# Two sums of a decode attention kernel, streamed through column tiles of the PE array instead of loaded as weights

## The chip, the cores and the metric

The kernel runs on one core of one Trainium2 chip. The metric is the device time of one execution in microseconds (us). Executions of one kernel agree within about 0.3%, so medians of several runs are given, and ratios with a 95% interval. A ratio is the mean time of one kernel's runs over the mean of the other's from the same rounds on the same chip, so it is not quite the ratio of the medians that stand beside it.

In the profiles PE is the matmul engine (TensorE) and PEld its weight loads, DVE is VectorE, ACT is ScalarE, POOL is GpSimd, and SP is SyncE, which issues most of the transfers here; `q` after a name means its instruction queue. SBUF is the on-chip memory, PSUM the one that matmuls write.

## The reference

The forward pass of a block for one decoded token, and its gradient with respect to everything. The part that matters:

```python
# x: [1, 1, 640]; k_cache, v_cache: [1, 32, 8192, 128] bf16 (32 heads, 8192 positions, 128 wide)
q = (xn @ wq)                                   # 32 heads of 128
scores = einsum("bhqd,bhkd->bhqk", q, k) * 128 ** -0.5
p = softmax(scores)
o = einsum("bhqk,bhkd->bhqd", p, v)             # "o sum"
out = x + o.reshape(...) @ wo + mlp(xn)         # ... cut
# and jax.vjp of this with grad_out. Per head, with do = wo-part of grad_out:
#   dv = p (outer) do;  ds = p * (do.v - sum(p * do.v));  dk = ds (outer) q;  dq = ds . k   # "dq sum"
```

K and V are read and dK and dV written once: 32 heads x 4 tensors of 2 MiB. That is 268 of the 305 MB that move.

## The kernel before

Position `s = 64 p + j` of a head lies on partition `p`, column block `j`, so a head's K or V is one SBUF tile of 128 partitions x 16 KiB. Ten such tiles (slots) circulate. Loads and stores of these tiles all go out on one queue (SP), in program order; a new load needs a slot whose store has landed:

```python
def store(kind, h):
    t = kv_tiles.pop((kind, h))
    # ... (cut)
    fifo((dkc if kind == "K" else dvc)[h], t[:])      # fifo = nc.sync.dma_start
    free_slots.append(t)
    load_next()                                       # loads into free_slots.pop(0)
```

PE transposes K and V in chunks (`T`, fp32 transposes of pairs of bf16, evicted from PSUM by ACT), and the transposed chunks are the weights of 64-column matmuls that give the scores and `do.v` (`M`). DVE writes the outer products dV and dK over the V and K tiles. The part that changes is the pair of sums over positions. It loads each 128x128 block of V (K) as weights and multiplies it by one column of p (ds), repeated over 64 columns:

```python
def o_sum(h, lo, hi):
    # ... (cut)
    for j in range(lo, hi):                            # 64 blocks in all
        nc.tensor.matmul(S_["hb"][:, 0:RW], lhsT=V3[:, j, :], rhs=S_["P2"][:, j, 0:1].to_broadcast([P, RW]),
                         start=(j == 0), stop=(j == J - 1), skip_group_check=True)

def dq_sum(h):
    # ... (cut)
    for j in range(J):
        nc.tensor.matmul(S_["hb"][:, RW:2 * RW], lhsT=K3[:, j, :], rhs=S_["U2"][:, j, 0:1].to_broadcast([P, RW]),
                         start=False, stop=(j == J - 1), skip_group_check=True)
    nc.scalar.copy(grp[g]["od"][:, hh, :], S_["hb"][:, RW - 1:RW + 1])
```

In a head the order was: `o_sum` first half, `dsum` (the scalar sum(p * do.v) for ds), `o_sum` second half, `dq_sum`.

## Time and profile before

749.35 us, median of 3 runs (748.56 to 749.82); the profiled execution spans 745.6 us.

| what | measured | where it is read |
|---|---|---|
| DMA share, 20 to 700 us | 0.99 to 1.02 | windows |
| PE / DVE / ACT busy | 80% / 60% / 45% | page, part 1 |
| SP waits for stores to land / for DVE's products | 544 us / 32 us | waits of SP |
| one DMA engine alone at the end | 731 to 744.2 us | windows |
| instructions of PE and PEld | 22,526 = 88.0 x 256 | page, part 1 |
| 16 KiB packets of the instruction queue q8 | 88 | page, part 3 |

The page of the kernel before: the span, busy times with instruction counts, the DMA's busy tenths and GB/s in 40 slices of 18.6 us, and the two queues that fetch instructions (packets, MB, share of 16 engines).

```profile
span 745.6 us, 25013 instructions
...
PE 596.1 (80%) x11263; PEld 568.4 (76%) x11263; DVE 447.8 (60%) x739; ACT 333.4 (45%) x668; POOL 30.4 (4%) x45
...
DMA  8999999999999999999999999999999999999991
GB/s 327 387 413 421 426 425 425 395 427 426 416 426 427 428 421 428 425 428 425 424 424 429 426 425 417 415 417 424 420 413 425 418 417 419 419 415 418 408 402 72
...
q8 instruction: 88, 1.44, 0.7%
...
q14 instruction: 20, 0.16, 0.1%
```

DMA is at 9 (90% or more) in every slice but the first and the last. "q8 instruction" and "q14 instruction" are not data: they are instructions being fetched.

The groups of instructions of the kernel before that the change touches or leans on: busy us and mean ns of one, then idle time before them and what ended it.

```profile
L274 PE MATMUL pT<-ident_f,kv 128*128 128x128 f32 x2048 | 337.1, 289 | 67.4 <-DMA kv<-in_A_k_cache_dram 62.4
L276 ACT COPY KT<-pT 128x512 f32<-128x512 f32 x512 | 299.3, 586 | 182.6 <-PE pT L274 149.4
...
L358 PE MATMUL hb<-P,kv 128*128 128x64 bf16 x2048 | 82.3, 202 | 14.3 <-DVE U L365 14.3
...
L373 PE MATMUL hb<-U,kv 128*128 128x64 bf16 x2048 | 70.8, 194 | 5.1 <-issue 5.1
```

A busy time of overlapping matmuls overstates their cost: in the timeline, from the start of a sum to the start of what PE does next, its 64 matmuls take 2.1 us (o, in two halves) and 1.95 us (dq). The first line shows PE idle for 62 us in front of transposes, waiting for K to arrive. PE waits for DMA, not the other way round.

The waits of the SP queue before (total us, times, longest), which issues the K and V transfers:

```profile
SPq L101 <- DMA out_dram<-kv: 543.6, 57, 16.9
SPq L101 <- DVE kv L379: 31.9, 11, 7.2
...
SPq L749 <- DMA out_dram<-fin_bf: 15.1, 1, 15.1
```

SP spends 544 us waiting for stores to land before it may reuse a slot, and only 32 us for DVE's outer products.

Windows of the kernel before. Columns: the stretch, its length, busy us and count of PE, PEld, DVE, ACT and POOL, the PE clock granted, the DMA share of 16 engines, GB/s.

```profile
300.00:320.00 20.00, 14.49 (x275) 13.84 (x274) 13.09 (x19) 8.93 (x18) 0.00 (x0) 0.98 1.01 427
720.00:731.00 11.00, 0.93 (x3) 0.59 (x3) 7.29 (x28) 0.00 (x0) 1.63 (x2) 0.50 0.85 346
731.00:736.00 5.00, 0.00 (x0) 0.00 (x0) 0.00 (x0) 0.00 (x0) 0.00 (x0) 0.50 0.06 26
736.00:741.00 5.00, 0.00 (x0) 0.00 (x0) 0.00 (x0) 0.00 (x0) 0.00 (x0) 0.50 0.06 25
```

A share of 0.06 is 1/16. From 731 us on one DMA engine works alone, at the 26 GB/s that one engine moves, with all other engines of the core finished. The timeline of the kernel before agrees (start, length, engine, instruction; the last three entries):

```profile
728.63 0.28 DVE L721 CAST fin_bf<-pT 10x128 bf16<-10x128 f32 x1 [0.56 <-PE pT L719]
728.94 0.54 ACTq L722 DMA_DIRECT2D out_dram<-fin_bf  x1
729.52 0.28 ACTq L723 DMA_DIRECT2D out_dram<-fin_bf  x1
```

The last result is sent at 729.8 us, 16 us before the end.

### The profile page before, as it was taken

What the parts mean: (1) busy time and instruction counts of PE and PEld (TensorE: products, weight loads), DVE (VectorE), ACT (ScalarE), POOL (GpSimd) and SP (SyncE); (2) the same over time, 40 slices, a digit from 0 to 9 for tenths busy, and PEclk for the clock granted to TensorE, in tenths of its full rate; (3) what the DMA queues carried; (4) which work ended last, traced back from release to release, by engine and by line L of the source; (5) the groups of instructions that cost most, each with busy time, mean ns of one, the idle gap of its engine ahead of it and who ended that gap; (6) DMA issues with size and microseconds to landing.
All of it is one profiled execution on the core that took longest, in us unless ns stands there. A gap on an engine that the chain in (4) does not pass through costs nothing.

```text
span 745.6 us, 25013 instructions
## 1 busy us (share of the span) xinstructions
PE 596.1 (80%) x11263; PEld 568.4 (76%) x11263; DVE 447.8 (60%) x739; ACT 333.4 (45%) x668; POOL 30.4 (4%) x45
## 2 busy tenths in 40 slices
PE   1987698999999779888787897778798788979920
PEld 1886598988998778877686896778798787869820
DVE  4169937677767456656555763646556664656580
ACT  1641055555565355535355553445454353554500
POOL 0100200000000100001000000000000000000000
PEclk9997799999999889999999999998999899988965
DMA  8999999999999999999999999999999999999991
GB/s 327 387 413 421 426 425 425 395 427 426 416 426 427 428 421 428 425 428 425 424 424 429 426 425 417 415 417 424 420 413 425 418 417 419 419 415 418 408 402 72
DMA packets 29136, 304.63 MB, mean 409 GB/s; under 512 B 2836, under 2 KB 5972, under 8 KB 12644
## 3 DMA queue, kind: packets, MB, share of 16 engines
q1 hardware_dynamic: 22736, 276.39, 88.5%
q0 software_dynamic: 5984, 26.30, 8.8%
q8 instruction: 88, 1.44, 0.7%
q10 hardware_dynamic: 308, 0.33, 0.1%
q14 instruction: 20, 0.16, 0.1%
HBM read 151.67 MB, written 151.34 MB: 406 GB/s over the span
## 4 chain that ended last, share of the span: by engine, by line
DMA 48%; PE 39%; DVE 8%; issue 2%; ACT 1%; SPq 0%; ACTq 0%; DVEq 0%
DMA kv<-in_A_k_cache_dram 31%; PE pT L274 17%; DMA out_dram<-kv 13%; PE hb L358 6%; PE hb L373 4%; PE sA L293 4%; DMA kv<-in_A_v_cache_dram 4%; PE dA L293 4%; DVE kv L379 3%; DVE U L365 1%; PE sA L320 1%; PE dh_ps L462 1%; PE hb L363 1%; PE acc L536 1%; PE gu_ps L451 1%
## 5 line engine op out<-in xcount | busy, mean ns | idle before, releaser
L274 PE MATMUL pT<-ident_f,kv 128*128 128x128 f32 x2048 | 337.1, 289 | 67.4 <-DMA kv<-in_A_k_cache_dram 62.4
L276 ACT COPY KT<-pT 128x512 f32<-128x512 f32 x512 | 299.3, 586 | 182.6 <-PE pT L274 149.4
L274 PEld LDWEIGHTS pT<-ident_f,kv 128*128 128x128 f32 x2048 | 224.6, 145 | 71.5 <-issue 69.6
L293 PEld LDWEIGHTS <-KT 128*128 128x128 bf16 x4096 | 196.8, 100 | 17.7 <-issue 10.6
L379 DVE TENSOR_TENSOR kv<-qd,U 128x4096 bf16<-128x4096 bf16 x64 | 146.0, 2284 | 0.0
L379 DVE TENSOR_TENSOR kv<-qd,P 128x4096 bf16<-128x4096 bf16 x64 | 143.4, 2282 | 0.0
L293 PE MATMUL dA<-cz,KT 128*128 128x64 bf16 x2048 | 107.6, 197 | 8.0 <-ACT qd L310 5.8
L293 PE MATMUL sA<-cz,KT 128*128 128x64 bf16 x2048 | 102.7, 192 | 0.4 <-issue 0.3
L358 PEld LDWEIGHTS <-kv 128*128 128x128 bf16 x2048 | 81.7, 106 | 16.5 <-issue 16.5
L358 PE MATMUL hb<-P,kv 128*128 128x64 bf16 x2048 | 82.3, 202 | 14.3 <-DVE U L365 14.3
L375 ACT COPY od_g<-hb 128x2 f32<-128x2 f32 x32 | 5.1, 160 | 160.9 <-PE hb L373 160.9
L373 PE MATMUL hb<-U,kv 128*128 128x64 bf16 x2048 | 70.8, 194 | 5.1 <-issue 5.1
L373 PEld LDWEIGHTS <-kv 128*128 128x128 bf16 x2048 | 66.9, 98 | 6.0 <-issue 5.8
L349 DVE SCALAR_TENSOR_TENSOR U<-dA,P 128x64 bf16<-128x64 f32 x32 | 7.4, 232 | 93.7 <-PE dA L293 93.7
L316 DVE TENSOR_REDUCE mrow<-sA 128x1 f32<-128x64 f32 x32 | 7.2, 224 | 79.5 <-PE sA L293 79.5
L365 DVE SCALAR_TENSOR_TENSOR U<-dA,hb,P 128x128 bf16<-128x128 f32 x32 | 11.4, 355 | 36.3 <-PE hb L363 36.3
L429 DVE SCALAR_TENSOR_TENSOR wq_g<-wq_g,side 128x512 bf16<-128x512 bf16 x40 | 27.3, 683 | 0.0
L340 DVE RECIPROCAL rZ<-sA 128x1 f32<-128x1 f32 x32 | 5.4, 168 | 35.9 <-PE sA L334 35.0
L233 DVE SCALAR_TENSOR_TENSOR side<-wo_g,g_bc 128x640 bf16<-128x640 bf16 x32 | 26.2, 818 | 0.3
L323 DVE TENSOR_REDUCE negM<-sA 128x1 f32<-128x128 f32 x32 | 9.3, 291 | 18.6 <-PE sA L320 18.6
L424 POOL DMA_DIRECT2D out_dram<-wo_g x8 | 6.1, 761 | 295.5 <-DVE cz L298 262.3
L433 POOL DMA_DIRECT2D out_dram<-wq_g x8 | 6.9, 863 | 254.3 <-DVE wq_g L431 254.3
(134 smaller groups left out, 311.5 us busy)
## 6 DMA issues: line engine op xcount, KB each, us to landing
out_dram<-kv SPq DMA_DIRECT2D x64, 2048.0 KB, 31.8
kv<-in_A_k_cache_dram SPq DMA_DIRECT2D x32, 2048.0 KB, 26.9
kv<-in_A_v_cache_dram SPq DMA_DIRECT2D x32, 2048.0 KB, 26.9
out_dram<-wo_g POOLq DMA_DIRECT2D x8, 640.0 KB, 12.1
out_dram<-wq_g POOLq DMA_DIRECT2D x8, 640.0 KB, 13.3
wq_g<-in_A_wq_dram POOLq DMA_DIRECT2D x7, 640.0 KB, 13.8
wo_g<-in_A_wo_dram POOLq DMA_DIRECT2D x7, 640.0 KB, 19.5
kv<-in_B_w_dram SPq DMA_DIRECT2D x2, 1728.0 KB, 16.1
```

The costliest lines, as they stand in the source:

```text
L233: nc.vector.scalar_tensor_tensor(junk[:], G_["wo"][:, hh, :], 1.0, g_bc[:], ALU.mult, ALU.mult, accum_out=G_["do"][:, hh:hh + 1])
L274: nc.tensor.transpose(pT[:, k * P:(k + 1) * P], W3[:, 4 * c + k, :], ident_f[:])
L276: nc.scalar.copy(KT[:].rearrange("p k w -> p (k w)"), pT[:])
L293: nc.tensor.matmul(S_[kind][:, 0:J], lhsT=KTb[:, k, par, :], rhs=S_["cz"][:, o:o + J], start=(i == 0 and par == 0), stop=(par == 1), skip_ ...
L320: nc.tensor.matmul(S_["K"][:, J:J + P], lhsT=S_["mrow"][:].to_broadcast([P, P]), rhs=ident_f[:], start=False, stop=True, skip_group_check= ...
L323: nc.vector.tensor_reduce(S_["negM"][:], S_["K"][:, J:J + P], AX.X, ALU.max, negate=True)
L358: nc.tensor.matmul(S_["hb"][:, 0:RW], lhsT=V3[:, j, :], rhs=S_["P2"][:, j, 0:1].to_broadcast([P, RW]), start=(j == 0), stop=(j == J - 1), ...
L363: nc.tensor.matmul(S_["hb"][:, 2 * RW:2 * RW + 1], lhsT=negones_b, rhs=S_["rdot"][:], start=False, stop=True, skip_group_check=True)
L365: nc.vector.scalar_tensor_tensor(S_["U2"][:], S_["V"][:, 0:J].unsqueeze(2).to_broadcast([P, J, 2]), S_["hb"][:, 2 * RW:2 * RW + 1], S_["P2 ...
L373: nc.tensor.matmul(S_["hb"][:, RW:2 * RW], lhsT=K3[:, j, :], rhs=S_["U2"][:, j, 0:1].to_broadcast([P, RW]), start=False, stop=(j == J - 1) ...
L379: nc.vector.tensor_tensor(dst[:, lo * DH:hi * DH].rearrange("p (j a b) -> p j a b", a=DH // 2, b=2), vec.rearrange("p (a b) -> p a b", b=2 ...
L429: nc.vector.scalar_tensor_tensor(wq_g[:, ci, :], wq_g[:, ci, :], 1.0, dqb, ALU.mult, ALU.mult, accum_out=dxa[:, ci, g:g + 1])
```

## The change

The intent is to shorten PE's work: V and K stream as the moving operand in 512-column matmuls, four columns of p (ds) are the weights, and four such matmuls are to run at once, one in each 32-column tile of the array. Row m of a result then holds column m of the weights against four blocks of V, of which only block m is wanted; that diagonal is picked out later, by fp32 matvecs with 0/1 masks, after ACT has evicted the PSUM tile.

```diff
-    def o_sum(h, lo, hi):          # 64 matmuls, V blocks as weights (cut)
+    def wsum(h, kind, pair):
+        N4 = 4 * DH
+        W = kv_tiles[(kind, h)]
+        X = pst()
+        nc.tensor.matmul(X[:], lhsT=cz_tiles[0][:, 0:1].to_broadcast([P, P]), rhs=W[:, 0:N4], start=True, stop=False,
+                         skip_group_check=True)                          # zero weights: clears all 128 rows
+        for i in range(J // 4):
+            q = QW * (i % 4)                                             # QW = 32
+            nc.tensor.matmul(X[q:q + 4, :], lhsT=pair[:, 4 * i:4 * i + 4, 0], rhs=W[:, N4 * i:N4 * (i + 1)],
+                             start=False, stop=(i >= J // 4 - 4), skip_group_check=True)
+        XS = kt_tile()
+        nc.scalar.copy(XS[:].rearrange("p k w -> p (k w)"), X[:])
+        hd[h]["xs" + kind] = XS
...
     def dq_sum(h):
-        ...                        # 64 matmuls, K blocks as weights (cut)
+        wsum(h, "K", hd[h]["U2"])
+
+    def col(h, kind):
+        ...
+        for r in range(4):
+            nc.tensor.matmul(S_["hb"][:, a:a + 1], lhsT=XS[:, r, :], rhs=mask4[:, r:r + 1],
+                             start=False, stop=(r == 3), skip_group_check=True)
+        if a:
+            nc.scalar.copy(grp[g]["od"][:, hh, :], S_["hb"][:, 0:2])
...
         rdot(h)
-        o_sum(h, 0, J // 2)
+        o_sum(h)
         dsum(h)
-        o_sum(h, J // 2, J)
+        if pre:
+            T(h + 1, "K", 2)
         dq_sum(h)
```

`col` runs inside the next head, between its first score chunks. Loads, stores and DVE's work are as before.

More of the change, by code (lines that the diff above doesn't have):

```diff
@@ L160 @@
     nc.vector.tensor_copy(ident_bf[:], ident_f[:])
-    pm_one = consts.tile([P, 2], F32, name="pm_one")
+    masks = consts.tile([P, 8], F32, name="masks")
+    pm_one = masks[:, 0:2]
     nc.vector.memset(pm_one[:, 0:1], 1.0)
@@ L170 @@
     HW = P // 2
-    mask2 = consts.tile([P, 2], F32, name="mask2")
-    nc.vector.tensor_reduce(mask2[:], ident_f[:].rearrange("p (a b) -> p a b", b=HW), AX.X, ALU.add)
+    mask2 = masks[:, 2:4]
+    nc.vector.tensor_reduce(mask2, ident_f[:].rearrange("p (a b) -> p a b", b=HW), AX.X, ALU.add)
+    QW = P // 4
+    mask4 = masks[:, 4:8]
+    nc.vector.tensor_reduce(mask4, ident_f[:].rearrange("p (a b) -> p b a", b=QW)[:, 0:4, :], AX.X, ALU.add)
     sel = consts.tile([P, 2, P], BF16, name="sel")
@@ L255, in prep_cm @@
                                 ps.unsqueeze(2).to_broadcast([P, 4 * GH, 2]),
-                                mask2[:].unsqueeze(1).to_broadcast([P, 4 * GH, 2]), ALU.mult)
+                                mask2.unsqueeze(1).to_broadcast([P, 4 * GH, 2]), ALU.mult)
     hd = {}
@@ L350, in rdot @@
                                        accum_out=S_["rdot"][:])
-    def o_sum(h, lo, hi):
-        S_ = hd[h]
-        if lo == 0:
-            S_["hb"] = ps_h.tile([P, 2 * RW + 1], F32, name="hb", tag="hb")
-        V3 = kv_tiles[("V", h)][:].rearrange("p (j d) -> p j d", d=DH)
-        for j in range(lo, hi):
-            nc.tensor.matmul(S_["hb"][:, 0:RW], lhsT=V3[:, j, :], rhs=S_["P2"][:, j, 0:1].to_broadcast([P, RW]),
-                             start=(j == 0), stop=(j == J - 1), skip_group_check=True)
+    def wsum(h, kind, pair):
[11 more added lines that the diff above has]
+        hd[h]["xs" + kind] = XS
@@ L361, in dsum, with o_sum @@
+    def o_sum(h):
+        wsum(h, "V", hd[h]["P2"])
     def dsum(h):
         S_ = hd[h]
-        nc.tensor.matmul(S_["hb"][:, 2 * RW:2 * RW + 1], lhsT=negones_b, rhs=S_["rdot"][:], start=False, stop=True,
+        S_["hb"] = ps_h.tile([P, 4], F32, name="hb", tag="hb")
+        nc.tensor.matmul(S_["hb"][:, 2:3], lhsT=negones_b, rhs=S_["rdot"][:], start=True, stop=True,
                          skip_group_check=True)
         nc.vector.scalar_tensor_tensor(S_["U2"][:], S_["V"][:, 0:J].unsqueeze(2).to_broadcast([P, J, 2]),
-                                       S_["hb"][:, 2 * RW:2 * RW + 1], S_["P2"][:], ALU.add, ALU.mult)
+                                       S_["hb"][:, 2:3], S_["P2"][:], ALU.add, ALU.mult)
@@ L368, in dq_sum @@
     def dq_sum(h):
+        wsum(h, "K", hd[h]["U2"])
+    def col(h, kind):
         g, hh = divmod(h, GH)
         S_ = hd[h]
-        K3 = kv_tiles[("K", h)][:].rearrange("p (j d) -> p j d", d=DH)
-        for j in range(J):
-            nc.tensor.matmul(S_["hb"][:, RW:2 * RW], lhsT=K3[:, j, :], rhs=S_["U2"][:, j, 0:1].to_broadcast([P, RW]),
-                             start=False, stop=(j == J - 1), skip_group_check=True)
-        nc.scalar.copy(grp[g]["od"][:, hh, :], S_["hb"][:, RW - 1:RW + 1])
+        XS = S_.pop("xs" + kind)
+        a = 0 if kind == "V" else 1
+        for r in range(4):
[3 more added lines that the diff above has]
+            nc.scalar.copy(grp[g]["od"][:, hh, :], S_["hb"][:, 0:2])
@@ L617, in head @@
         has_prev = h > 0 and h != MLP_AT
-        had = 2 if h != MLP_AT else 0
+        had = (3 if h else 2) if h != MLP_AT else 0
         if nxt:
@@ L623, in head @@
         side_k(h)
+        if had == 3:
+            M(h, "K", 0)
         for c in range(had, NCH):
@@ L627, in head @@
                 M(h, "K", c - 2)
+            if has_prev and c == 3:
+                col(h - 1, "V")
+            if has_prev and c == 4:
+                col(h - 1, "K")
         T(h, "V", 0)
@@ L663, in head @@
         rdot(h)
-        o_sum(h, 0, J // 2)
+        o_sum(h)
         dsum(h)
-        o_sum(h, J // 2, J)
+        if pre:
+            T(h + 1, "K", 2)
         dq_sum(h)
+        if not pre:
+            col(h, "V")
+            col(h, "K")
     prep_new(0)
```

## The prediction

> **What bounds it now.** DMA. In the windows view the DMA share is 0.99 to 1.02 from 20 us to 700 us, at 398 to 432 GB/s, while PE is 80% busy and DVE 60%. PE sits idle 62 us in front of its transposes for K loads (groups view, L274). The SP queue waits 544 us for stores of K and V tiles before it may load again (waits of SP), and about 32 us for DVE's outer products.
>
> The end is peculiar. The last compute is at 729 us, the two tiny result stores go out at 729.5, yet the span is 745.6. From 731 to 744.6 the windows show DMA share 0.06 and 27 GB/s: one of 16 engines alone, finishing the last V and K stores in 16 KiB packets of 0.61 us. I put its extra work on PE's instruction fetch: queue 8 carries 88 packets of 16,384 bytes, each about 1.0 us. The Trainium skill, "Runtime: NRT & Kernel Launch", section "Instruction fetch mechanics", says refills are 16 KiB blocks of 256 instructions; the trace agrees: PE and PEld have 22,526 instructions, 88.0 blocks. Most fetches overlap one data packet lengthened by 0.3 to 0.6 us; 88 x about 0.38 us (estimate) = 33 us extra for that engine.
>
> **What the change does, per head.**
> - Removes 128 matmuls of 64 columns with their weight loads: 2.1 us for o and 1.95 us for dq in the chain.
> - Adds 2 zeroing matmuls and 32 four-wide ones over 512 columns. From L462 (384 columns, 0.266 us apart at clock 0.67) I estimate 0.24 us per 512 columns at full clock. Four tiles at once: 5 passes, 1.2 us per sum; serial: 17 passes, 4 us. The skill, "TensorE: Matmul & The Clock Gate", Part 3, gives 2.38x for three column tiles; no trace here shows it yet. I expect overlap, 1.2 to 1.8 us per sum.
> - Adds 8 fp32 mask matvecs, two passes each, at 0.12 us per fp32 pass (four transposes take 0.47 us): 1.9 us.
> - Adds two 128x512 evictions on ACT, 0.586 us each: 37 us in all, ACT 333 to about 370.
> - Moves one transpose chunk between the sums. DVE work, DMA bytes and load order stay.
>
> So PE gains no busy time (estimate 4.3 to 5.5 us against 4.05 per head), and it is off the critical path: a head needs about 17.5 us of PE against 21 us of DMA. What shrinks is the instruction stream: 22,526 to about 17,530, 88 to about 68.5 fetch blocks. 19.5 blocks x 0.38 us = 7 us off the lone engine's tail. The others end near 731 us: the floor.
>
> **Predicted: 742 us, range 735.5 to 750 (80%).** Faster by over 2%: 0.06. Within 2%: 0.87. Slower by over 2%: 0.07.
>
> **What would show it.** Right: queue 8 near 69 packets; the lone-engine stretch shrinks from 13.6 us to about 7; DMA share stays 1.0 at about 425 GB/s in the middle; PE busy within 10% of 596 us; DVE unchanged; each sum takes 1.2 to 1.8 us.
> Wrong: the lone-engine tail stays at 14 us with 69 fetches (fetch is not its cause); DMA share below 0.95 in the middle (PE or ACT paces it).
>
> **What would make it wrong.** If column tiles do not overlap, PE needs 22 to 23 us per head, more than DMA's 21: slower by 2 to 5%. Drains at mode switches, or XS tiles held across heads crowding the four-deep transpose ring, act the same way. If the lone engine was not always busy, the 7 us shrink towards 0.

## More of the kernel before

The MLP's forward and gradient run once, between heads 1 and 2; its gradients go out on POOL's queue.

The trace does not name the engine of a packet.

## The result, and the profile after

744.56 us, median of 6 runs (742.3 to 745.32), against 749.0 us (747.93 to 749.82) for the kernel before: ratio 0.9937, 95% interval 0.9922 to 0.9953. The 4.7 us are clear of noise.

The page of the kernel after, the lines that answer to those above:

```profile
span 743.1 us, 20151 instructions
...
PE 607.7 (82%) x8767; PEld 512.8 (69%) x8767; DVE 447.5 (60%) x740; ACT 370.9 (50%) x732; POOL 30.4 (4%) x45
...
DMA  8999999999999999999999999999999999999992
GB/s 320 384 408 419 422 425 428 352 428 421 406 424 431 425 423 427 426 427 426 424 428 426 428 426 425 426 427 426 424 427 426 420 424 423 418 423 421 421 404 92
...
q8 instruction: 69, 1.13, 0.6%
...
q14 instruction: 21, 0.17, 0.1%
```

PE is busier (608 against 596 us), ACT too (371 against 333), DVE as before, and DMA is at 9 throughout. What fell is the number of PE instructions, and with it q8: 69 packets instead of 88.

The new groups of the kernel after:

```profile
L368 ACT COPY KT<-pT 128x512 f32<-128x512 f32 x64 | 37.5, 586 | 74.0 <-PE pT L365 45.9
...
L391 PE MATMUL hb<-masks,KT 128*128 128x1 f32 x512 | 65.8, 250 | 0.0
...
L365 PE MATMUL pT<-kv,P 128*4 128x512 bf16 x512 | 41.6, 455 | 0.0
L365 PE MATMUL pT<-kv,U 128*4 128x512 bf16 x512 | 33.1, 379 | 0.4 <-DVE U L379 0.4
L361 PE MATMUL pT<-kv,cz 128*128 128x512 bf16 x64 | 27.6, 432 | 0.0
```

One head's PE work in the timeline of the kernel after:

```profile
301.62 0.38 PE L361 MATMUL pT<-kv,cz 128*128 128x512 bf16 x1
301.93 1.03 PE L365 MATMUL pT<-kv,U 128*4 128x512 bf16 x16
...
303.85 1.03 PE L391 MATMUL hb<-masks,KT 128*128 128x1 f32 x8
```

16 matmuls of 512 columns take 1.03 us, the zeroing one 0.3 us before them, and the four fp32 mask matvecs of a sum (8 passes) 1.0 us. Two sums with their masks cost about 4.6 us of PE, against 4.05 us before. The change does not save PE time at all.

The waits of SP after, and windows of the kernel after (columns as before):

```profile
SPq L101 <- DMA out_dram<-kv: 556.8, 57, 16.3
SPq L101 <- DVE kv L398: 25.6, 5, 8.5
...
SPq L778 <- DMA out_dram<-fin_bf: 15.2, 1, 15.2
```

```profile
131.00:135.00 4.00, 4.00 (x67) 3.94 (x66) 2.22 (x2) 2.87 (x6) 0.00 (x0) 1.00 0.78 268
300.00:320.00 20.00, 15.00 (x226) 12.84 (x225) 13.24 (x21) 10.34 (x21) 0.00 (x0) 0.99 1.02 430
720.00:731.00 11.00, 0.93 (x3) 0.59 (x3) 5.54 (x24) 0.00 (x0) 0.86 (x1) 0.50 0.74 296
731.00:736.00 5.00, 0.00 (x0) 0.00 (x0) 0.00 (x0) 0.00 (x0) 0.00 (x0) 0.50 0.06 25
736.00:741.00 5.00, 0.00 (x0) 0.00 (x0) 0.00 (x0) 0.00 (x0) 0.00 (x0) 0.50 0.06 26
```

The middle (300 to 320 us) runs at the full DMA rate, as before. At the end one engine is again alone, to 741.6 us instead of 744.2. The first window is new: between 131 and 135 us the DMA share falls to 0.78, the slice of 352 GB/s in the page; the kernel before has only a dip to 395 there.

### The profile page after: what moved, and what is told of

Same layout as the page of the kernel before. It is cut to its first block, busy times and chain, and to the rows that moved or that the text cites. A ratio compares the mean times of both kernels' runs of the same rounds, so it can differ in the third digit from the quotient of the medians.

```text
span 743.1 us, 20151 instructions
## 1 busy us (share of the span) xinstructions
PE 607.7 (82%) x8767; PEld 512.8 (69%) x8767; DVE 447.5 (60%) x740; ACT 370.9 (50%) x732; POOL 30.4 (4%) x45
## 4 chain that ended last, share of the span: by engine, by line
DMA 61%; PE 28%; DVE 6%; issue 1%; ACT 1%; SPq 0%; DVEq 0%; ACTq 0%
DMA kv<-in_A_k_cache_dram 27%; DMA out_dram<-kv 26%; PE pT L279 12%; DMA kv<-in_A_v_cache_dram 8%; PE pT L365 3%; PE sA L298 3%; PE dA L298 3%; DVE kv L398 3%; PE hb L391 2%; PE pT L361 1%; PE dh_ps L481 1%; PE hb L377 1%; PE acc L555 1%; PE sA L325 1%; DVE kv L558 1%
## 5 line engine op out<-in xcount | busy, mean ns | idle before, releaser
L281 ACT COPY KT<-pT 128x512 f32<-128x512 f32 x512 | 299.1, 586 | 213.8 <-PE pT L279 187.4
L279 PEld LDWEIGHTS pT<-ident_f,kv 128*128 128x128 f32 x2048 | 234.5, 150 | 77.8 <-issue 75.7
L298 PEld LDWEIGHTS <-KT 128*128 128x128 bf16 x4096 | 194.7, 100 | 28.3 <-issue 21.4
L368 ACT COPY KT<-pT 128x512 f32<-128x512 f32 x64 | 37.5, 586 | 74.0 <-PE pT L365 45.9
L391 PE MATMUL hb<-masks,KT 128*128 128x1 f32 x512 | 65.8, 250 | 0.0
L391 PEld LDWEIGHTS hb<-masks,KT 128*128 128x128 f32 x512 | 62.0, 192 | 0.9 <-issue 0.9
L365 PE MATMUL pT<-kv,P 128*4 128x512 bf16 x512 | 41.6, 455 | 0.0
L365 PE MATMUL pT<-kv,U 128*4 128x512 bf16 x512 | 33.1, 379 | 0.4 <-DVE U L379 0.4
L361 PE MATMUL pT<-kv,cz 128*128 128x512 bf16 x64 | 27.6, 432 | 0.0
L365 PEld LDWEIGHTS <-P 128*4 128x4 bf16 x512 | 10.3, 90 | 22.1 <-issue 12.7
L377 PEld LDWEIGHTS hb<-rdot,masks 128*128 128x128 f32 x64 | 11.0, 216 | 17.8 <-issue 17.8
```

The costliest lines, as they stand in the source:

```text
L279: nc.tensor.transpose(pT[:, k * P:(k + 1) * P], W3[:, 4 * c + k, :], ident_f[:])
L281: nc.scalar.copy(KT[:].rearrange("p k w -> p (k w)"), pT[:])
L298: nc.tensor.matmul(S_[kind][:, 0:J], lhsT=KTb[:, k, par, :], rhs=S_["cz"][:, o:o + J], start=(i == 0 and par == 0), stop=(par == 1), skip_ ...
L361: nc.tensor.matmul(X[:], lhsT=cz_tiles[0][:, 0:1].to_broadcast([P, P]), rhs=W[:, 0:N4], start=True, stop=False, skip_group_check=True)
L365: nc.tensor.matmul(X[q:q + 4, :], lhsT=pair[:, 4 * i:4 * i + 4, 0], rhs=W[:, N4 * i:N4 * (i + 1)], start=False, stop=(i >= J // 4 - 4), sk ...
L368: nc.scalar.copy(XS[:].rearrange("p k w -> p (k w)"), X[:])
```

## The experiments

Theory A is that of the prediction: instruction fetch loads one DMA engine, that engine's total work sets the time, and the change helps because it issues fewer instructions. Rival B is that the new PE work or its order is what helps; rival C, that PE time counts.

### e1_pad: the changed kernel with its instruction count brought back

```diff
+    def pad(h, kind, pair, js):
+        W3 = kv_tiles[(kind, h)][:].rearrange("p (j d) -> p j d", d=DH)
+        for j in js:
+            nc.tensor.matmul(hd[h]["hb"][:, 3:4], lhsT=W3[:, j, :], rhs=pair[:, j, 0:1],
+                             start=False, stop=True, skip_group_check=True)
...
         dsum(h)
+        pad(h, "V", hd[h]["P2"], range(39))
...
         dq_sum(h)
+        pad(h, "K", hd[h]["U2"], range(39))
```

> The changed kernel with 78 dummy matmuls of one column per head (each with its weight load), 39 after each sum, into an unused PSUM column: PE plus PEld back to 22,526 instructions, 88 fetch blocks instead of 69, about 2.4 us more PE time per head. Result stays correct. Theory A (instruction fetch loads one DMA engine): time goes back to about 749, ratio to before 0.998 to 1.002, queue 8 at 88 packets, lone-engine stretch longer by 1.5 to 5 us. Rival B (the gain came from PE work and its order, the column-tile algorithm itself): if PE has slack, the time stays at 744 to 745 (ratio 0.993 to 0.995).

Measured: 749.13 us against 748.48, ratio 1.0005 (0.9993 to 1.0018). q8 is back at 88 packets. The whole gain is gone, as A says. Three lines of e1_pad, of its page, its windows (columns as before) and its timeline, and the same last result in the changed kernel:

```profile
q8 instruction: 88, 1.44, 0.7%
...
710.00:715.00 5.00, 5.00 (x87) 4.74 (x84) 2.34 (x5) 4.01 (x9) 0.00 (x0) 1.00 0.30 120
...
738.11 0.28 DVE L758 CAST fin_bf<-pT 10x128 bf16<-10x128 f32 x1 [0.56 <-PE pT L756]
...
726.84 0.28 DVE L750 CAST fin_bf<-pT 10x128 bf16<-10x128 f32 x1 [0.56 <-PE pT L748]
```

The lone-engine stretch got shorter, though (from 739.0 to 745.6 us, by the trace's packets), because the other engines end 9 us later than in the changed kernel: here PE is late at the end (busy all of 710 to 715 us, with a DMA share of 0.30), and the last compute is at 738 us instead of 727. So e1_pad's time alone does not rule out that late PE work set it. The trace's packets speak against that: between 712 and 725 us, where the other DMA engines have long idle stretches, at least one packet of data is always under way, and for 4.7 us in sum exactly one. It looks as if one engine had a backlog throughout. The length of the stretch is the wrong thing to watch; the lone engine's finish is the right one.

### e2_time: the same PE time in few instructions

```diff
+        for i in range(n):               # n = 5 after dsum, 6 after dq_sum; hb widened to 512 columns
+            nc.tensor.matmul(hd[h]["hb"][:, 4:508], lhsT=W[:, i * DH:(i + 1) * DH], rhs=W[:, 1024:1528],
+                             start=False, stop=True, skip_group_check=True)
```

> The changed kernel with 11 dummy matmuls of 504 columns per head (about 2.4 us of PE time per head as in the one-column padding, but only 22 instructions per head, 704 in all, 2.75 fetch blocks). Result stays correct. Theory A: 744.5 to 745.5, ratio 0.993 to 0.996. Rival C (extra PE time, not extra instructions, is what costs): as slow as the one-column padding, about 749.

Measured: 743.9 us, ratio 0.9936 (0.9923 to 0.9948). PE is 653 us busy here and 657 us in e1_pad, and the two differ by 5.2 us. PE time up to 88% costs nothing; rival C falls. The pair is not a pure comparison of instruction counts, though: with nearly the same busy time the last compute is at 729.0 us here and at 738.1 in e1_pad.

### e3_cut and e8_cut2: the kernel before with fewer instructions and nothing else

```diff
-        for j in range(lo, hi):
+        for j in [j for j in range(lo, hi) if (25 * j) % J < 25]:      # e3_cut: 25 of 64; dq_sum likewise
+        for j in [j for j in range(lo, hi) if j in (0, J // 2)]:       # e8_cut2: 2 of 64
```

The results are wrong on purpose.

> The kernel before with 25 of the 64 matmuls left in each of the o and dq sums (wrong result on purpose): PE plus PEld 17,534 instructions as in the changed kernel, 69 fetch blocks, none of the new algorithm, no extra ACT evictions. Theory A: the whole gain appears, 744 to 745, ratio 0.992 to 0.995. Rival B (the new algorithm or its order is the cause): stays at 748 to 749.5; if lighter PE alone lets loads start sooner, below 743.

> The kernel before with 2 of the 64 matmuls left in each sum (wrong result on purpose): PE plus PEld 14,590 instructions, 57 fetch blocks, 31 fewer than before, 12 fewer than with 25 matmuls left. Theory A at 0.36 us per block: 11 us off, 737 to 738.5, ratio 0.984 to 0.987, lone-engine stretch down to about 4 us. If the gain is not proportional to fetch blocks but comes from something in the first cut (lighter PE with a floor), it stays at 741 to 742.

Measured: e3_cut 741.45 us, ratio 0.9910 (0.9897 to 0.9924); e8_cut2 737.92 us, ratio 0.9857 (0.9844 to 0.9871). Rival B falls: nothing of the new algorithm is needed. But e3_cut is below 743, where its expectation puts another rival, that lighter PE alone lets loads start sooner: these two runs take away PE work (551 and 513 us busy, against 596) together with instructions (e11_pool_pad, below, does not). Of e8_cut2's expectation the time was right and the lone-engine stretch of about 4 us wrong: 8.2 us by the trace's packets. The line of q8 in the page of e8_cut2, 57 packets:

```profile
q8 instruction: 57, 0.93, 0.5%
```

| pair | fetch blocks between them | difference | per block |
|---|---|---|---|
| before, e3_cut | 19.5 | 6.7 us | 0.35 us |
| e3_cut, e8_cut2 | 11.5 | 4.0 us | 0.35 us |
| e2_time, e1_pad | 16.75 | 5.2 us | 0.31 us |
| e9_after_again, e11_pool_pad (below) | 12.5 | 4.2 us | 0.34 us |

(Blocks: the difference in instructions / 256. Difference: that of the ratios, times the median of the kernel before in those rounds.) The prices agree at about 0.33 us per 16 KiB of instructions. The intervals of the ratios leave each difference 1.0 to 1.4 us either way, so this is agreement within about a third, and no more. Only the last pair leaves PE's work as it was. e3_cut did better than expected, and better than the changed kernel with as many PE instructions; that is taken up below. Part of the two cuts' gain may lie elsewhere: in the first 100 us of their traces the 16 engines have about 15 us in sum without a packet, against 26 us before, which is under 1 us for one engine.

### e11_pool_pad: instructions on another engine's stream

```diff
+        for _ in range(100):                      # at the start of each head
+            nc.gpsimd.memset(idle[:], 0.0)        # idle: one element
```

> The changed kernel with 100 one-element POOL memsets at the start of each head: 3,200 more instructions, 12.5 blocks, on POOL's stream and none on PE's. If every engine's instruction fetch loads the same DMA engine: 4 us slower than the changed kernel, about 748.5, ratio near 1.000. If POOL's instructions are fetched by another DMA engine, which has slack until about 730 us: unchanged at 744 to 745, ratio 0.993 to 0.995, queue 8 still at 68 or 69.

Measured: 748.66 us, ratio 1.0008 (0.9995 to 1.0022), where the changed kernel had 0.9952 on the same chip. Its page:

```profile
q8 instruction: 68, 1.11, 0.6%
...
q14 instruction: 46, 0.38, 0.1%
```

q8 did not move, but q14 has 46 packets where the changed kernel had 21: 25 more of 8,192 bytes, which is 3,200 x 64 bytes. Within the intervals they cost as much per byte as PE's. So PE's stream is not special: POOL's counts too; PE's just has most of the instructions. This is the cleanest of the tests, as PE, DVE and ACT do what they did. (POOL is 43% busy here instead of 4%, and its own DMA issues could come later; but the middle's DMA rate is nearly the same, 426 GB/s at 300 to 320 us, and SP waits as before, 557 us for stores and 27 us for DVE's products.)

### e4_k8 and e12_five: which engine, and is it really one?

e4_k8 stores the last K tile as 16 stores of 8 partitions:

```diff
+        if kind == "K" and h == H - 1:
+            for p0 in range(0, P, 8):
+                fifo(dkc[h][p0:p0 + 8, :], t[p0:p0 + 8, :])
```

> The changed kernel with the last K store issued as 16 stores of 8 partitions each. By the Trainium skill page on DMA each such store runs on 8 engines, the lowest-numbered; then engines 0 to 7 carry 16 packets of this tile instead of 8 and engines 8 to 15 none. One tile is 8 packets of 0.61 us, 4.9 us. If the lone engine is among 8 to 15, the end comes about 4.9 us sooner (about 739.5); if it is among 0 to 7, about 4.9 us later (about 749.5). If the last stretch is not one engine's backlog but something else, unchanged at 744 to 745.

Measured: 756.3 us, ratio 1.0101 (1.0088 to 1.0115): slower, as for an engine among 0 to 7, but by 12 us more than the changed kernel and not by 4.9. The windows of e4_k8 show why this run can't be read that way:

```profile
730.00:733.00 3.00, 0.00 (x0) 0.00 (x0) 0.00 (x0) 0.00 (x0) 0.00 (x0) 0.50 0.16 40
741.00:751.00 10.00, 0.00 (x0) 0.00 (x0) 0.00 (x0) 0.00 (x0) 0.00 (x0) 0.50 0.45 95
```

Until 733 us nearly only the late engine works; then eight engines move the pieces at 95 GB/s in sum instead of 8 x 26. SP's timeline shows one reason: the 16 pieces went out one by one from 716 to 748 us, where the changed kernel issues its one store at 716.3 us. So their end follows from when they were issued too. The run is inconclusive on which engine it is.

e12_five asks the same without touching the end: 8 extra copies of 5 rows into a scratch buffer in HBM, in the middle of the run.

```diff
+        if kind == "K" and 8 <= h < 24 and h % 2 == 0:
+            i = (h - 8) // 2
+            fifo(scratch[10 * i:10 * i + 10:2, :], kc[h][0:10:2, :])
```

> The changed kernel with 8 extra copies of 5 rows of 16 KiB each (heads 8 to 22, on the SP queue, into a scratch buffer in HBM): 0.66 MB more, 0.2% of the bytes, but by the Trainium skill page on DMA each copy of 5 rows runs on 5 engines only, the lowest-numbered, one packet of 16 KiB each; so 8 packets more for each of engines 0 to 4. In the trace before, one packet of the five-row result store sits inside the lone engine's chain of packets, so the lone engine should be one of these five. If the end is that one engine's backlog: 8 x 0.61 = 4.9 us slower than the changed kernel, about 749.5, ratio about 1.000 to 1.003, lone-engine stretch longer by about 5 us. If the end is set by total bytes or by all engines together: 8 x 5 packets over 16 engines, 1.5 us at most, about 746. If the lone engine is not among the five: unchanged, since the others have 10 us of slack.

Measured: 749.71 us, ratio 1.0022 (1.0006 to 1.0039): 5.2 us over the changed kernel's 744.56, and 5.2 to 6.4 us by the ratios, for 0.2% more bytes. The windows of e12_five near the end, and its last result in the timeline:

```profile
736.00:741.00 5.00, 0.00 (x0) 0.00 (x0) 0.00 (x0) 0.00 (x0) 0.00 (x0) 0.50 0.06 25
741.00:745.00 4.00, 0.00 (x0) 0.00 (x0) 0.00 (x0) 0.00 (x0) 0.00 (x0) 0.50 0.07 29
...
731.79 0.28 DVE L755 CAST fin_bf<-pT 10x128 bf16<-10x128 f32 x1 [0.56 <-PE pT L753]
```

The lone engine works to 746.0 us here, 741.6 in the changed kernel. The expected growth of the lone-engine stretch by 5 us did not come (13.4 us by the trace's packets, 11.7 in the changed kernel), because the rest is later too: the last compute is at 731.8 us instead of 726.8, though the last of the copies was issued at 560 us and no compute was added. So a few engines with more to carry hold back the whole kernel. (Issuing the eight copies took SP 0.7 us each; it waits 553 us for stores, so that is not what costs.) The Trainium skill, "DMA: Bandwidth & Descriptors", section "Why a DMA increments its semaphore by 16 and not by 1", says that a DMA issued from SP runs on k engines, k being the largest number up to 16 that divides the slowest dimension of both its sides, and that these are the lowest-numbered ones. The run agrees as far as it can: five rows load an engine that the end depends on, by 8 packets of 0.61 us. Which of the five it is stays open.

### e7_one_tile: no overlap between the column tiles

```diff
-            q = QW * (i % 4)
+            q = 0
```

> The changed kernel with all 16 accumulating matmuls of each sum in the first 32-column tile, so that none can overlap another; result stays correct, instruction count unchanged. If column tiles overlap in the changed kernel (16 in about 1.0 us), each sum grows here to 3.5 to 4 us, PE by about 5 us per head, and PE takes over from DMA: 760 to 785, DMA share below 0.97 in the middle. If they did not overlap, unchanged at 744.

Measured: 803.91 us, ratio 1.0747 (1.0726 to 1.0767); slower than expected. One sum in the timeline of e7_one_tile:

```profile
301.88 0.38 PE L361 MATMUL pT<-kv,cz 128*128 128x512 bf16 x1
302.19 3.62 PE L365 MATMUL pT<-kv,U 128*4 128x512 bf16 x16
```

16 matmuls take 3.62 us in one tile and 1.03 us in four: 3.5 times faster for four. The Trainium skill, "TensorE: Matmul & The Clock Gate", Part 3, gives 2.38 times for three column tiles; this trace is in line with it and adds the figure for four. Without overlap PE becomes the limit, as the page and the waits of SP show:

```profile
span 803.1 us, 20151 instructions
...
PE 740.8 (92%) x8767; PEld 556.4 (69%) x8767; DVE 447.6 (56%) x740; ACT 369.7 (46%) x732; POOL 30.4 (4%) x45
```

```profile
SPq L101 <- DVE kv L398: 445.0, 46, 11.9
...
SPq L101 <- DMA out_dram<-kv: 55.7, 7, 17.1
```

SP no longer waits for stores (56 us) but for DVE's products (445 us), which wait for PE. The overlap saves 5.2 us per head, 166 us in all; the kernel without it is 59 us slower, so the rest would have been slack.

### e5_mlp_sp, e6_before_mlp_sp: the stall near 131 us

The changed kernel gains 4.7 us, and 19.5 blocks at 0.33 us make 6.4. The stall near 131 us was a candidate: SP waits there 16 us for a store before its next load, while the MLP's gradient stores, issued from POOL, are under way. Both kernels were run with these stores on SP's queue.

```diff
-        nc.gpsimd.dma_start(dv[:, 0:NA, :], wa)       # and four more stores of mlp()
+        nc.sync.dma_start(dv[:, 0:NA, :], wa)
```

> The changed kernel with the five MLP gradient stores issued on the SP queue instead of POOL's. Around 131 to 141 us the changed kernel's DMA falls to about 150 to 280 GB/s: SP waits 16 us for a store before its next load (until 133.5 us) while the POOL-issued MLP stores, in 6,912-byte packets, take 37 us to land; half the engines run dry. If that stall costs the changed kernel 2 to 2.5 us, which it does not cost the padded version, it vanishes here: about 742, ratio to before 0.989 to 0.992, GB/s over 410 in every slice from 3 to 36. If the stall is not made by these stores, or is made up later, unchanged at 744 to 744.5.

> The kernel before with the same five stores on the SP queue. Its own dip at this place was small (395 GB/s in one slice, about 1.2 us of an engine). Expected 747 to 748.5, ratio 0.997 to 1.000; then the gap between the two SP-queue versions is the fetch saving alone, 6 to 7 us. If instead this gains as much as the changed kernel does, the stall does not explain why the change got only 4.7 us.

Measured: e5_mlp_sp 744.03 us, ratio 0.9941 (0.9928 to 0.9955); e6_before_mlp_sp 749.28 us, ratio 1.0011 (0.9998 to 1.0023). The stall is gone (between the third slice and the last the lowest of e5_mlp_sp is 398 GB/s), and the time is unchanged: of the two outcomes expected, the second. e6_before_mlp_sp is a little above its range. The gap between the two versions is 5.2 us, against 4.7 us (3.6 in e9_after_again, below) between the kernels as they are. That puts the stall at 0.5 to 1.6 us, but the intervals leave about 1.8 us either way: it may cost nothing, or most of what is missing.

### e9_after_again: the changed kernel once more

> The changed kernel once more, unaltered, on the chip of the next two. 743.5 to 745, ratio to before 0.992 to 0.995, with a second look at its DMA stall near 131 to 135 us: if that is part of the program it is there again (a slice at 350 to 360 GB/s), if it is chance it is not, and then the lone engine should end 1 to 2 us earlier.

Measured: 744.84 us against 748.36, ratio 0.9952 (0.9938 to 0.9965), 3.6 us. The stall is there again, 339 GB/s in the same slice, so it belongs to the program. The change is thus worth 3.6 to 4.7 us.

### e10_merged: a version with fewer instructions still

Both sums share one PSUM tile (o in column tiles 0 and 1, dq in 2 and 3), so one zeroing matmul and one eviction serve both; masks and evicted sums are bf16, and each of 4 mask matvecs gives o and dq in two columns.

```diff
-        X = pst()                                    # and zeroing, for each sum
+        a = 0 if kind == "V" else 2                  # X made and zeroed for V only
-            q = QW * (i % 4)
+            q = QW * (a + i % 2)
-        XS = kt_tile()                               # fp32, for each sum
+        if a:                                        # once, bf16
+            XS = t_tile()[:, 0:N4].rearrange("p (k w) -> p k w", w=P)
...
-            nc.tensor.matmul(S_["hb"][:, a:a + 1], lhsT=XS[:, r, :], rhs=mask4[:, r:r + 1],
+            nc.tensor.matmul(S_["hb"][:, 0:2], lhsT=XS[:, r, :], rhs=mask4[:, r, :],
```

> A version meant to be better than both: o uses column tiles 0 and 1, dq tiles 2 and 3, of one PSUM tile, so one zeroing matmul and one ACT eviction serve both, and the masks and the evicted sums are bf16, one pass for each of 4 two-column matvecs. PE plus PEld 16,702 instructions, 65.2 blocks, 3.3 fewer than the changed kernel; ACT evictions 32 instead of 64. Result correct. Theory A at 0.33 us per block: 1.1 us below the changed kernel, 743 to 743.5, ratio 0.991 to 0.993. Each sum takes about 1.9 us instead of 1.05 with two tiles in place of four; if PE time mattered this would be slower than the changed kernel instead.

Measured: correct, 742.28 us (741.23 to 742.83), ratio 0.9917 (0.9902 to 0.9931), on the same chip where the changed kernel had 744.84; the time is 0.7 us below the range expected. It beats both kernels, by 2.6 us more than the change, of which 3.3 blocks explain 1.1. Its slice near 131 us is at 396 GB/s, so it does not have the stall; that may be the rest, or the 21 us less of ACT work, but neither was tried alone. With two column tiles each sum overlaps less, and nothing is lost by it.

## Why the prediction was right or wrong

- **DMA bounds the kernel, and PE, DVE and ACT are off the critical path: right.** The share stayed at 1.0 in the middle, and e2_time added 45 us of PE busy time for nothing. Whether the change's 37.5 us more of ACT cost anything was not tried alone.
- **The time, 742 us (735.5 to 750): right within the range**, 2.6 us low. "Within 2%" held. The range also holds the 749 us of no change at all, so the hit by itself says little; the queue 8 count and the experiments carry the argument.
- **The mechanism: that fewer instruction bytes are what helps is shown**, by putting them on another engine (e11_pool_pad), with taking them away (e3_cut, e8_cut2) and putting them back (e1_pad) in agreement, all near 0.33 us per block. That an engine among five sets the end is shown by e12_five: bytes put on those five cost about what they cost on one engine. That the fetches load this same engine is argued from both together, since the trace does not name a packet's engine. One thing stays open in it: 16 KiB of instructions cost 0.33 us, 16 KiB of data on the five engines 0.65 to 0.8 us (5.2 to 6.4 us for 8 packets). In the trace before, 81 data packets of 16 KiB that overlap a fetch took at least 0.3 us longer than the usual 0.61 us. They lie at 62 of the 88 fetches, where 1 us stretches taken at random meet such a packet in 28% of cases; 108 more packets were as late with no fetch beside them, so fetches are not the only cause of late packets.
- **The size, "19.5 blocks x 0.38 us = 7 us off the lone engine's tail": too large.** It measured 4.7 and 3.6 us. The price per block was 0.33 us (6.4 us for 19.5); the remaining 2 to 3 us the changed kernel gives back somewhere. The stall near 131 us may account for some of them (0.5 to 1.6 us, 1.8 us either way). The rest is not settled; it is as small as the intervals.
- **"The lone-engine stretch shrinks from 13.6 us to about 7": wrong.** By the trace's packets it went from 13.1 to 11.7 us (9.8 in e9_after_again). The step that failed is the sentence "The others end near 731 us: the floor". The others are no fixed floor: SP lets a load go only when an older store has landed, which is when its slowest engine has written its part; so a late engine can hold the others back too (e12_five shows it: 5 us later compute from bytes on five engines), and with fewer fetches all of them finish sooner. In e8_cut2 the others were done at 725.6 us by the trace's packets, well below that "floor".
- **Queue 8 near 69 packets, ACT about 370 us, PE busy within 10% of 596, DVE unchanged: right** (69, 371, 608, 447.5).
- **The sums, 1.2 to 1.8 us each, if the tiles overlap: right** (1.3 us with the zeroing, or 1.0 without), and the masks, 1.9 us: right (2 x 1.0). **Without overlap "slower by 2 to 5%": mis-sized**; e7_one_tile was 7.5% slower.

## What to carry to other kernels

When DMA is busy all the time, look at who shares it: here each 16 KiB of instructions, of PE or of POOL, cost about 0.33 us, most likely because their fetches fall on one of the data engines, and a tile is free only when its slowest engine has stored its part. Then count instructions, not engine time: a change that leaves PE as busy as it was can still gain, and one that issues more instructions, on POOL too, can lose. A DMA share of 1/16 at the end of a run is the sign to look for.

## What the Trainium skill lacked or had wrong

- "Runtime: NRT & Kernel Launch", "Instruction fetch mechanics": it calls the cost of crossing a 16 KiB boundary "mostly hidden". In this kernel, which DMA bounds, it was not: 0.31 to 0.35 us per 16 KiB in four pairs of runs, 29 us for PE's 88 blocks if scaled (an estimate). The section gives the fetches no cost in DMA time.
- The same section gives blocks of 16 KiB. PE's came in packets of 16,384 bytes (88 for 22,526 instructions); POOL's 3,200 extra instructions came in 25 packets of 8,192.
- "TensorE: Matmul & The Clock Gate", Part 3, has three column tiles (2.38 times) and no figure for four of 128x32: 16 matmuls of 512 columns took 1.03 us in four tiles, 3.62 us in one, 3.5 times.
